# A planned order fitted anew: the planner counts TensorE's changes between full and half-array products, and has new lengths for attention's products

## The chip, the cores and the metric

The kernel runs on one core of a Trainium2 chip. The number to explain is the device time of one execution in microseconds. Before the change three runs took 861.77, 862.43 and 864.25 us; their median is 862.43.

The core's engines each take their own instructions strictly in order: TensorE (PE, matrix products; its weight loads are shown as PEld), VectorE (DVE), ScalarE (ACT), GpSimd (POOL), and SyncE (SP), which here only issues transfers. They meet through semaphores: an instruction that waits holds everything behind it on its engine.

## The reference

Attention with a window of 128 keys and a distance penalty per head, then two layers of a pair of products with a gate between them:

```python
# q, k, v: 4 batches, 8 heads, 576 positions, 64 per head
scores = scale * np.matmul(q, k.transpose(0, 1, 3, 2))
mask = (rel >= 0) & (rel < window)                       # window = 128
scores = np.where(mask, scores + bias[None], -1000000000.0)
attn = np.exp(scores - max) ; attn = attn / (sum + 1e-09)
x = matmul(attn, v), heads side by side                  # 2304 tokens x 512
h = x @ w_in ; g = h * np.tanh(softplus(h)) ; x = g @ w_out     # layer 0, d_ff 2048
h = x @ w_in ; g = np.where(h > 0, h, np.exp(h) - 1) ; x = g @ w_out   # layer 1
```

## The kernel before, in words

**The products.** Each of the four products of the two layers (2304 x 512 x 2048 and its counterpart) is done by a scheme of seven block products in place of eight (STEPS P1 to P7), with sums and differences of blocks of the operands and the results on DVE, ACT and POOL. Every operand is split into a high part in the short fp32r format and a low rest, and each block product is three matmuls (high-high, high-low, low-high). The inward products of layer 0 have 288 columns (tiles hA, hB, hC; `hidden`), those of layer 1 and both outward products 384 (tiles hA, hB, hC and oA, oB, oC; `hidden`, `outward`). One planned PE operation is a block of 6 (hidden) or 12 (outward) matmuls.

**Attention** is cut into 48 units (`unit`): batch, pair of heads, and one of three parts of the positions. A unit has scores (tile ps_s), a softmax on DVE and ACT (p, st), one or two transposes (ps_t, L822), masked copies (pt, L852), and values (ps_o, L870). The scores of parts 0 and 1 (L767) use 64 of the array's 128 rows, for two heads side by side; the values use 64 of its columns; scores of part 2 (L755), transposes and all products of the layers use the whole array. Going from one of these three ways to another is what the change calls a change of mode.

**Weights** come packed. They are joined from two words (raw, bits; L633 to L646), summed (sums), and split (w); those of layer 0's inward product stay on the core, the others go out to memory and come back later. Between the two products of a layer the gate (graw) goes through memory as well; its activation in layer 0 (L1020) needs another table of ACT than the joining of weights does (L635), and each alternation is an ACT_TABLE_LOAD.

**Stages.** Batch 0's attention runs first; from then on the attention of the next batch is interleaved with the hidden products of the one before (batches 0 to 3). The hidden products of batch 3 have no attention beside them. Then come layer 0's outward products (three blocks of 768 tokens), layer 1's hidden ones (three blocks) and layer 1's outward ones.

**Who sets the order.** The code first records every operation with its engine or engines, its modelled cost, what it reads and writes and when it is due (`Plan.op`, called by `pe`, `act`, `dve`, `dma`, `copy`, `combine`). `Plan.rank_all` gives each a priority: the due time of its users less its modelled step, plus the number that the table SHIFT has for its group (unit, weight tile, block product). `Plan.order` then plays the operations through on modelled engines: whenever an engine is free, it takes the ready operation of the lowest rank, and where several engines can do it, the one that would be done first. The instructions are emitted in the order so found; the modelled times themselves leave no trace in the program. When PE finds nothing ready in its model before the time AT["fill"] (90 us), it takes an unused product (L531: 256 columns in bf16, on a constant, which nobody reads), which keeps the engine active. The costs of PE's operations are written beside them: `pe(cost, ...)` at L755, L767, L822 and L870 for attention.

## Time and profile before

| | |
|---|---|
| median of three runs | 862.43 us (861.77 to 864.25) |
| the profiled execution | 861.93 us, its span 860.2 us |
| granted TensorE clock | 1.00 in every stretch looked at (of 2.4 GHz) |
| PE busy | 836.7 us, 97% of the span |
| DVE busy | 731.5 us, 85% |
| ACT busy | 617.9 us, 72% |
| POOL busy | 116.2 us, 14% |

A stretch is read by comparing its length with what each engine was busy in it. Ends of matmuls are modelled and matmuls overlap, so PE's busy time is at most a hint; the time from the start of one block of products to the start of the next is exact. A number in brackets at a row's end is the engine's idle time before it and what ended that idle time.

### The profile page before, as it was taken

The numbers are of one execution on the slowest core, as the hardware profiler recorded it, in microseconds if no ns is written. First come the engines' busy times: TensorE is split into PE (matmuls) and PEld (weight loads), VectorE is DVE, ScalarE is ACT, GpSimd is POOL, SyncE is SP. The second block draws the span as 40 slices with busy tenths as digits, with TensorE's granted clock in tenths as the row PEclk, the third lists the DMA queues.
The fourth block names the chain that finished last, engine by engine and source line by source line (L and its number), as shares of the span: only waits on it lengthen the run. The fifth ranks groups of instructions, "written<-read, shape, count | busy, mean of one in ns | idle before, by whom it ended". The sixth has DMA issues, their size and how long they took to land.

```text
span 860.2 us, 15671 instructions
## 1 busy us (share of the span) xinstructions
PE 836.7 (97%) x5394; PEld 790.2 (92%) x5394; DVE 731.5 (85%) x1629; ACT 617.9 (72%) x1397; POOL 116.2 (14%) x104
## 2 busy tenths in 40 slices
PE   9999999999999999999899999999999998999998
PEld 6777788888889999999899999999999998999998
DVE  8999997888888789998899988986787997887863
ACT  6989887778788879885986667987699763322442
POOL 0432101112101000345200323221000000000000
PEclk9999999999999999999999999999999999999999
DMA  7346648997988996864874877793367937236001
GB/s 279 126 134 223 224 161 250 320 307 243 315 281 285 337 314 240 273 214 136 284 254 133 273 245 269 256 320 142 142 215 249 357 137 255 92 110 225 33 19 55
DMA packets 85967, 187.66 MB, mean 218 GB/s; under 512 B 8577, under 2 KB 30081, under 8 KB 85889
## 3 DMA queue, kind: packets, MB, share of 16 engines
q1 hardware_dynamic: 85888, 186.68, 64.1%
q8 instruction: 42, 0.69, 0.3%
q14 instruction: 37, 0.29, 0.1%
HBM read 117.44 MB, written 69.21 MB: 217 GB/s over the span
## 4 chain that ended last, share of the span: by engine, by line
PE 60%; DMA 13%; DVE 12%; ACT 7%; issue 6%; POOL 1%; SPq 1%; ACTq 0%; DVEq 0%; POOLq 0%
PE hA L956 20%; PE hC L956 10%; PE oA L1043 9%; PE oC L1043 5%; PE hB L956 5%; DMA graw<-gate 4%; DVE hl L576 3%; PE ps_o L870 3%; DMA qkv<-in_qkv_dram 3%; PE ps_s L767 2%; DVE graw L576 2%; DMA raw<-in_w_dram 2%; DVE w L576 2%; PE oB L1043 2%; PE ps_t L822 2%
## 5 line engine op out<-in xcount | busy, mean ns | idle before, releaser
L956 PE MATMUL hA<-xt,w 128*128 128x288 f32 (+1 forms) x1344 | 231.5, 317 | 3.4 <-ACT g L571 1.8
L1043 PE MATMUL oA<-hl,w 128*128 128x384 f32 x1152 | 215.9, 338 | 5.8 <-DVE hl L576 3.7
L956 PEld LDWEIGHTS hA<-xt,w 128*128 128x128 f32 x1344 | 207.3, 188 | 9.7 <-ACT g L571 3.6
L1043 PEld LDWEIGHTS oA<-hl,w 128*128 128x128 f32 x1152 | 202.7, 188 | 9.2 <-DVE hl L576 6.5
L571 ACT ACTIVATE hl<-graw 128x768 fp32r<-128x768 f32 x145 | 121.1, 842 | 111.1 <-PE oA L1043 58.0
L576 DVE TENSOR_TENSOR hl<-graw,hl 128x768 fp32r<-128x768 f32 x168 | 166.6, 1005 | 28.4 <-ACT hl L571 27.7
L956 PE MATMUL hC<-xt,w 128*128 128x288 f32 (+1 forms) x672 | 119.3, 317 | 1.0 <-ACT xc L571 1.0
L1043 PE MATMUL oC<-hl,w 128*128 128x384 f32 x576 | 108.8, 339 | 1.7 <-DVE hl L576 1.0
L956 PEld LDWEIGHTS hC<-xt,w 128*128 128x128 f32 x672 | 104.3, 188 | 3.7 <-ACT xc L571 1.3
L1043 PEld LDWEIGHTS oC<-hl,w 128*128 128x128 f32 x576 | 101.6, 188 | 3.1 <-DVE hl L576 2.0
L576 DVE TENSOR_TENSOR graw<-graw 128x768 f32<-128x768 f32 x96 | 92.6, 980 | 9.0 <-DMA graw<-gate 4.7
L646 POOL TENSOR_TENSOR bits<-bits,raw 128x512 int32<-128x512 int32 x30 | 47.7, 1591 | 296.0 <-DVE bits L643 176.0
L571 ACT ACTIVATE g<-hA 128x288 f32<-128x288 f32 (+1 forms) x144 | 60.7, 434 | 22.7 <-PE hA L956 20.4
L787 ACT ACTIVATE p<-p,st 128x128 f32<-128x128 f32 x144 | 56.2, 395 | 10.6 <-DVE st L783 10.4
L956 PE MATMUL hB<-xt,w 128*128 128x288 f32 (+1 forms) x336 | 60.5, 316 | 0.4 <-ACT g L571 0.4
L576 DVE TENSOR_TENSOR w<-w 128x512 fp32r<-128x512 f32 x84 | 56.7, 698 | 1.6 <-ACT w L571 1.5
L1043 PE MATMUL oB<-hl,w 128*128 128x384 f32 x288 | 54.3, 338 | 1.1 <-DVE hl L576 1.1
L956 PEld LDWEIGHTS hB<-xt,w 128*128 128x128 f32 x336 | 52.7, 188 | 1.2 <-ACT g L571 0.8
L571 ACT ACTIVATE w<-w 128x512 fp32r<-128x512 f32 x82 | 49.5, 625 | 4.3 <-DMA w<-w_out 3.1
L1043 PEld LDWEIGHTS oB<-hl,w 128*128 128x128 f32 x288 | 50.8, 188 | 1.4 <-DVE hl L576 1.4
L938 ACT ACTIVATE e<-e 128x384 f32<-128x384 f32 x96 | 48.9, 536 | 0.6
L802 ACT ACTIVATE p<-p,st 128x128 f32<-128x128 f32 x124 | 41.1, 396 | 8.9 <-DVE st L797 8.8
(99 smaller groups left out, 1114.9 us busy)
## 6 DMA issues: line engine op xcount, KB each, us to landing
graw<-gate SPq DMA_DIRECT2D x96, 384.0 KB, 5.9
raw<-in_w_dram SPq DMA_DIRECT2D x64, 512.0 KB, 5.5
gate<-g SPq DMA_DIRECT2D x64, 288.0 KB, 4.5
gate<-g SPq DMA_DIRECT2D x48, 384.0 KB, 3.6
w<-w_out SPq DMA_DIRECT2D x56, 256.0 KB, 4.8
qkv<-in_qkv_dram SPq DMA_DIRECT2D x16, 512.0 KB, 5.4
w_out<-bits SPq DMA_DIRECT2D x32, 256.0 KB, 4.8
w<-w_in SPq DMA_DIRECT2D x28, 256.0 KB, 3.1
```

Of the source, the lines that this page charges most:

```text
L571: ways = [("act", act_cost(n, sbuf), lambda: nc.scalar.activation(o(), i(), AF.Copy), 0.0), ("dve", dve_cost(n, sbuf), lambda: nc.vector.t ...
L576: emit = lambda eng: eng.tensor_tensor(out=o(), in0=x(), in1=y(), op=op)
L646: add = lambda eng, raw=raw, bits=bits: eng.tensor_tensor(out=bits().bitcast(I32), in0=bits().bitcast(I32), in1=raw()[:, :, 0].bitcast(I32 ...
L767: nc.tensor.matmul(pss[j]()[:, n, w0:2 * P], qs()[rs, n * P:(n + 1) * P], ks()[rs, ko + w0:ko + 2 * P], start=n == 0, stop=True, skip_grou ...
L787: act(P, lambda n=n, j=j: nc.scalar.activation(prob()[:, n, j], prob()[:, n, j], AF.Exp, scale=-1.0, bias=st()[:, 0, n, j:j + 1], accum_ou ...
L802: ("act", act_cost(P, True, 1), lambda y=y, f=f: nc.scalar.activation(y(), y(), AF.Copy, scale=f()), AT["norma"]),
L822: nc.tensor.transpose(ps()[:, j], prob()[:, n, j], ident)
L870: nc.tensor.matmul(o()[j * D:(j + 1) * D, c0:c0 + math.prod(y.shape[1:])], vn()[:kr, n, j], y, start=n == 0, stop=n == nkb - 1, skip_group ...
L938: act(T, lambda: nc.scalar.activation(e(), e(), AF.Relu, scale=-1.0, bias=1.0), (), [e], due)
L956: nc.tensor.matmul(ps(), w()[:, a, wi, cs], x()[:, b, k], start=step in FIRST and k == 0 and m == 0, stop=k == 1 and m == 2, skip_group_ch ...
L1043: nc.tensor.matmul(bk[name, d](), w()[:, a, wi, cs], x()[:, b, k], start=step in FIRST and f + k == 0 and m == 0, stop=f + k == NQ - 1 and ...
```

## The change

The planner now knows three modes of PE's operations: 0 (whole array), 1 (scores of parts 0 and 1), 2 (values). An operation in another mode than the last one costs SWITCH = 0.09 us more in the model, and its rank is worse by AT["mode"] = 3.5. The modelled lengths of attention's products are replaced by others, each shorter: scores 0.95 and 1.16 us become 0.76 and 0.97, those of part 2 0.33 become 0.19; a pair of transposes 0.22 becomes 0.14; values of parts 0, 1 and 2 0.90, 1.16 and 0.58 become 0.715, 0.93 and 0.44. With these costs the table SHIFT (over 500 numbers) and six numbers of AT were fitted again. No operation of the computation is added or taken away.

```diff
@@ -19,106 +19,109 @@
-AT = dict(copy=2.27, both0=-0.71, both1=-8.32, both2=-3.61, turn=7.60436, held=102.159, fill=90, enough=1.5, norma=-0.5,
-          normp=2.42, kappa=1.35238, lag=0.940919, first=-64.52, unit=2.69, h1=50.67, chunk=70.1, lead=30.24, dt=1.35,
-          dma=-7.29047, conv=-27.63, wadd=-0.1, soft0=0, soft1=0, soft2=0, soft3=0, eq=4, ep=2, et=6, er=3, eb=0,
-          eraw=3, side0=1, side1=2, depth=4, ahead=-153.07, hb=5, lrot=2)
+AT = dict(copy=2.27, both0=-0.71, both1=-8.32, both2=-3.61, turn=2.59709, held=117.913, fill=90, enough=1.5, norma=-0.5,
+          normp=2.42, kappa=1.33691, lag=0.880417, first=-64.52, unit=2.69, h1=50.67, chunk=70.1, lead=30.24, dt=1.35,
+          dma=-5.30616, conv=-27.63, wadd=-0.1, soft0=0, soft1=0, soft2=0, soft3=0, eq=4, ep=2, et=6, er=3, eb=0,
+          eraw=3, side0=1, side1=2, depth=4, ahead=-161.724, hb=5, lrot=2, mode=3.49599)
 SHIFT = {
-    "H000P1": -15.5, "H000P2": 52.4, "H000P3": -45.1, "H000P4": -13.3, "H000P5": -21, "H000P6": -39.5, "H000P7": -1.9,
...
+    "H000P1": -19.1, "H000P2": -27.5, "H000P3": -67, "H000P4": -32.8, "H000P5": -26.3, "H000P6": -65.3, "H000P7": 0.1,
...
@@ -148,6 +151,7 @@
     WARM = 4.0
     START = dict(pe=0.75, act=1.9, dve=2.6, pool=2.6, sp=0.6)
     LOAD = 1.3
+    SWITCH = 0.09
     RATE, OUTSTANDING, LANDING = 390e3, 8, 1.9
     def __init__(self):
@@ -178,7 +182,7 @@
                 return t + span
             t = (k + 1) * self.TICK + 1e-9
-    def op(self, ways, reads=(), writes=(), at=None, due=None, moved=0, rows=1.0, table=None, port=False):
+    def op(self, ways, reads=(), writes=(), at=None, due=None, moved=0, rows=1.0, table=None, port=False, mode=0):
         deps, bufs = set(), {}
         me = len(self.ops)
         for what, wr in [(x, False) for x in reads] + [(x, True) for x in writes]:
@@ -200,7 +204,7 @@
             b.left += 1
             b.ops.append(me)
         self.ops.append(dict(group=self.group, ways=ways, deps=deps, bufs=list(bufs), at=at, due=due, moved=moved, rows=rows,
-                             table=table, port=port))
+                             table=table, port=port, mode=mode))
     def rank_all(self):
         ops = self.ops
@@ -248,7 +252,7 @@
         events = sorted(free.values())
         dma_free = held_until = 0.0
         landed = []
-        loaded = "exp"
+        loaded, mode = "exp", 0
         self.columns = {}
         out = []
@@ -261,7 +265,8 @@
         def rank(e):
             held = AT["held"] * (e == "dve" and free["pool"] > t + 0.3)
-            return lambda i: (ops[i]["prio"] + AT["turn"] * turns(i) + held * ops[i]["port"], i)
+            return lambda i: (ops[i]["prio"] + AT["turn"] * turns(i) + held * ops[i]["port"] +
+                              (AT["mode"] if e == "pe" and ops[i]["mode"] != mode else 0.0), i)
         def finish(e, cost, i, t):
             ahead = 0.0
@@ -314,6 +319,7 @@
                             out.append(self.fill[1])
                         else:
                             continue
+                        mode = 0
                         free[e] = self.clocked(t, self.fill[0], 1.0)
                         self.fills.append((t, free[e]))
                         heapq.heappush(events, free[e])
@@ -334,7 +340,10 @@
                         at = max(t, held_until)
                     if o["moved"] and len(landed) >= self.OUTSTANDING:
                         at = max(at, landed[-self.OUTSTANDING])
-                    end = self.clocked(t, way[1], o["rows"]) if e == "pe" else at + way[1] + self.LOAD * turns(best)
+                    if e == "pe":
+                        switch = self.SWITCH * (o["mode"] != mode)
+                        mode = o["mode"]
+                    end = self.clocked(t, way[1] + switch, o["rows"]) if e == "pe" else at + way[1] + self.LOAD * turns(best)
                     loaded = o["table"] or loaded
                     late = self.LATENCY[e]
                     self.log.append((e, best, at, end))
@@ -561,8 +570,8 @@
     def dve(n, emit, reads, writes, due, fast=False, extra=0, port=False):
         plan.op([("dve", dve_cost(n, fast, extra), emit, 0.0)], reads, writes, due=due, port=port or fast)
-    def pe(cost, emit, reads, writes, at, rows=1.0):
-        plan.op([("pe", cost + 0.003, emit, 0.0)], reads, writes, at=at, rows=rows)
+    def pe(cost, emit, reads, writes, at, rows=1.0, mode=0):
+        plan.op([("pe", cost + 0.003, emit, 0.0)], reads, writes, at=at, rows=rows, mode=mode)
     def dma(moved, emit, reads, writes, due, slow=1.0):
         plan.op([("sp", 0.43, emit, 0.0)], reads, writes, due=due, moved=moved * slow)
@@ -752,7 +761,7 @@
             if part == 2:
                 ps = buf(ring, (512,), F32, "ps_s")
                 r = rows(4)
-                pe(0.0017 * nk, lambda: nc.tensor.matmul(ps()[:, :nk], qs(), ks(), start=True, stop=True), [t], [ps], at)
+                pe(0.001 * nk, lambda: nc.tensor.matmul(ps()[:, :nk], qs(), ks(), start=True, stop=True), [t], [ps], at)
                 dve(r, lambda: nc.vector.copy_predicated(ps()[:, :r], own[:, :r], ps()[:, P:P + r]), ["own"], [ps], due)
                 heads = [(0, 0, lambda: ps()[:, :P], relt[:, pr], ("relt", pr), ps)]
             else:
@@ -767,7 +776,7 @@
                             nc.tensor.matmul(pss[j]()[:, n, w0:2 * P], qs()[rs, n * P:(n + 1) * P], ks()[rs, ko + w0:ko + 2 * P],
                                              start=n == 0, stop=True, skip_group_check=True)
-                pe((0.66 if part == 0 else 0.87) + 0.29, mm, [t], list(pss), at, rows=0.8)
+                pe(0.76 if part == 0 else 0.97, mm, [t], list(pss), at, rows=0.9, mode=1)
                 for j, ps in enumerate(pss):
                     if part == 0:
                         dve(P, lambda ps=ps: nc.vector.copy_predicated(
@@ -821,7 +830,7 @@
                 for j in range(w):
                     nc.tensor.transpose(ps()[:, j], prob()[:, n, j], ident)
-            pe(0.109 * w, mm, [(prob, (n, j)) for j in range(w)], [ps], at)
+            pe(0.108 * w - 0.08, mm, [(prob, (n, j)) for j in range(w)], [ps], at)
             if part == 2:
                 from_, mask = (lambda kr: ps()[:kr, 0].rearrange("p (j q) -> p j q", j=2)), keep[:, :, :TAIL]
                 dst = lambda pt, x, kr: pt()[:kr, x, 0].rearrange("p (j q) -> p j q", j=2)
@@ -871,9 +880,9 @@
                                          start=n == 0, stop=n == nkb - 1, skip_group_check=True)
             cols = 2 * TAIL if part == 2 else P * sum(w for _, w, _, _ in places)
-            cost = 0.00175 * cols + 0.03 * nkb + (0.3 if part == 2 else 0.17)
+            cost = (0.715, 0.93, 0.44)[part]
             pe(cost, mm, [(pts[pt], x) for x0, w, _, pt in places for x in range(x0, x0 + (1 if part == 2 else w))] + [t],
-               [o], at, rows=0.0018 * cols / cost)
+               [o], at, rows=min(1.0, 0.0018 * cols / cost), mode=2)
             x, k = xc
             copy(nq, lambda: x()[:, k, q0:q0 + nq], lambda: o()[:, :nq], [o], [[(x, k, 0)], [(x, k, 1), (x, k, 2)], [(x, k, 3)]][part],
                  at + 2, sbuf=False)
```

Counted over the whole orders: PE's products of the computation are the same; the unused products are 193 where there were 146, of which 175 (140) stand ahead of the first hidden product and 18 (6) behind it; changes of mode are 137 where there were 134; ACT's table loads behind the first are 12 where there were 14. Some operations that more than one engine can do have moved between DVE, ACT and POOL.

First place, PE, from attention of batch 0 to the first hidden product (hA). Before:

```order
L767 MATMUL ps_s<-qkv 128x128 x2
L767 MATMUL ps_s<-qkv 128x256 x2
L870 MATMUL ps_o<-pt,qkv 64x64 x4
L870 MATMUL ps_o<-pt,qkv 64x256 x2
L870 MATMUL ps_o<-pt,qkv 64x128 x4
L870 MATMUL ps_o<-pt,qkv 64x256 x2
L870 MATMUL ps_o<-pt,qkv 64x128 x2
L956 MATMUL hA<-xt,w 128x288 x6
L531 LDWEIGHTS const-bfloat16-1.0
L531 MATMUL unused<-const-bfloat16-1.0 128x256
```

In the change:

```order
L879 MATMUL ps_o<-pt,qkv 64x256 x2
L879 MATMUL ps_o<-pt,qkv 64x128 x2
L965 MATMUL hA<-xt,w 128x288 x6
L776 MATMUL ps_s<-qkv 128x128 x2
L776 MATMUL ps_s<-qkv 128x256 x2
L879 MATMUL ps_o<-pt,qkv 64x64 x4
L965 MATMUL hC<-xt,w 128x288 x6
L965 MATMUL hB<-xt,w 128x288 x6
L965 MATMUL hA<-xt,w 128x288 x6
L776 MATMUL ps_s<-qkv 128x256 x4
L540 LDWEIGHTS const-bfloat16-1.0
L540 MATMUL unused<-const-bfloat16-1.0 128x256
```

A scores step and a values step of 64 columns, which stood close ahead of the first hidden block, now stand behind it; the six unused products (each with its weight load) that stood right behind the first hA block now stand behind later scores (7 of them there, and 4 and 7 more behind the next hC blocks).

Second place, ACT in layer 0's outward stage, second block of tokens (graw: activation of the gate, L1020, L1029 in the change; raw: joining of weights, L635, L639, in the change L644, L648; hl: high part of an operand). Before:

```order
L639 ACTIVATE raw<-raw 128x512
L635 ACT_TABLE_LOAD
L635 ACTIVATE raw<-raw 128x512
L1020 ACT_TABLE_LOAD
L1020 ACTIVATE graw<-graw 128x768 x2
L571 ACTIVATE hl<-graw 128x768 x2
L639 ACTIVATE raw<-raw 128x512
L1020 ACTIVATE graw<-graw 128x768
L635 ACT_TABLE_LOAD
L635 ACTIVATE raw<-raw 128x512
L571 ACTIVATE hl<-graw 128x768 x2
L1020 ACT_TABLE_LOAD
```

In the change:

```order
L1029 ACT_TABLE_LOAD
L1029 ACTIVATE graw<-graw 128x768 x4
L580 ACTIVATE hl<-graw 128x768
L1029 ACTIVATE graw<-graw 128x768 x3
L580 ACTIVATE hl<-graw 128x768
L1029 ACTIVATE graw<-graw 128x768
L580 ACTIVATE hl<-graw 128x768 x3
L648 ACTIVATE raw<-raw 128x512
L644 ACT_TABLE_LOAD
L644 ACTIVATE raw<-raw 128x512
L580 ACTIVATE hl<-graw 128x768
L644 ACTIVATE raw<-raw 128x512
```

The activations of the gate, which alternated with single conversions and their tables, now stand together behind one load; the conversions follow behind the next.

Third place, DVE in layer 1's outward stage, first block of tokens, from taking the results out of banks oB to those of oA (y), with the sums of the gate's blocks (graw) and the low parts of operands (hl). Before:

```order
L576 TENSOR_TENSOR y<-oB,y 128x384 x2
L576 TENSOR_TENSOR hl<-graw,hl 128x768
L576 TENSOR_TENSOR graw<-graw 128x2x384
L576 TENSOR_TENSOR hl<-graw,hl 128x768
L576 TENSOR_TENSOR graw<-graw 128x2x384
L576 TENSOR_TENSOR hl<-graw,hl 128x768
L576 TENSOR_TENSOR graw<-graw 128x2x384
L576 TENSOR_TENSOR hl<-graw,hl 128x768
L576 TENSOR_TENSOR y<-oA,y 128x384 x2
L576 TENSOR_TENSOR hl<-graw,hl 128x768
```

In the change:

```order
L585 TENSOR_TENSOR y<-oB,y 128x384
L585 TENSOR_TENSOR hl<-graw,hl 128x768
L585 TENSOR_TENSOR y<-oB,y 128x384
L585 TENSOR_TENSOR w<-w 128x512
L585 TENSOR_TENSOR graw<-graw 128x2x384
L585 TENSOR_TENSOR hl<-graw,hl 128x768 x2
L585 TENSOR_TENSOR y<-oA,y 128x384 x2
L585 TENSOR_TENSOR hl<-graw,hl 128x768
```

Between the two, DVE had three sums of graw and four low parts; now it has one sum, the low part of a weight tile and two low parts (and one between the two takings of oB).

## Rows read from the trace of the kernel before

**Rows 1.** One line of the page: busy us (share of the span) x instructions.

```profile
PE 836.7 (97%) x5394; PEld 790.2 (92%) x5394; DVE 731.5 (85%) x1629; ACT 617.9 (72%) x1397; POOL 116.2 (14%) x104
```

**Rows 2.** Stretches: window, length; busy us (count) of PE, PEld, DVE, ACT, POOL; clock; DMA.

```profile
0.00:44.20 44.20, 42.20 (x368) 30.99 (x368) 40.16 (x205) 36.71 (x133) 11.62 (x19) 1.00 0.58 204
44.20:120.00 75.80, 70.11 (x546) 59.65 (x544) 71.84 (x261) 67.38 (x212) 17.39 (x15) 1.00 0.60 199
120.00:264.70 144.70, 142.29 (x1124) 124.56 (x1123) 124.04 (x457) 111.87 (x359) 18.60 (x17) 1.00 0.81 267
...
309.75:497.00 187.25, 182.42 (x1025) 179.59 (x1024) 174.49 (x214) 149.31 (x210) 41.49 (x28) 1.00 0.70 234
497.00:673.50 176.50, 175.37 (x995) 173.78 (x994) 142.46 (x252) 144.98 (x318) 27.04 (x25) 1.00 0.68 233
673.50:856.60 183.10, 179.27 (x1010) 176.68 (x1008) 144.58 (x182) 71.94 (x103) 0.00 (x0) 1.00 0.39 136
```

**Rows 3.** The chain that ended last, in order of time: start us, us, what.

```profile
733.51 10.53 PE oA L1043 x60
```

**Rows 4.** PE in order of time, 112 to 122 us: start us, us, what, count.

```profile
117.05 0.60 PE L870 MATMUL ps_o<-pt,qkv 128*64 128x64 f32 x8
117.58 1.07 PE L956 MATMUL hC<-xt,w 128*128 128x288 f32 x6
118.48 0.96 PE L956 MATMUL hB<-xt,w 128*128 128x288 f32 x6
119.28 0.96 PE L956 MATMUL hA<-xt,w 128*128 128x288 f32 x6
120.17 1.14 PE L767 MATMUL ps_s<-qkv 64*128 64x256 f32 x8
121.23 0.93 PE L956 MATMUL hC<-xt,w 128*128 128x288 f32 x5
```

**Rows 5.** The same view around the first hidden product; in brackets idle time before.

```profile
35.05 3.19 PE L531 MATMUL unused<-const-bfloat16-1.0 128*128 128x256 bf16 x27
38.08 0.27 PE L822 MATMUL ps_t<-ident,p 128*128 128x128 f32 x1
...
44.21 1.06 PE L956 MATMUL hA<-xt,w 128*128 128x288 f32 x6
45.11 0.84 PE L531 MATMUL unused<-const-bfloat16-1.0 128*128 128x256 bf16 x6
46.94 1.07 PE L956 MATMUL hC<-xt,w 128*128 128x288 f32 x6 [0.99 <-ACT xc L571]
```

**Rows 6.** DVE's groups by line and form: count | busy us, mean ns | idle before.

```profile
L576 DVE TENSOR_TENSOR w<-bits,w 128x512 fp32r<-128x512 f32 x11 | 8.5, 773 | 0.0
...
L646 DVE CUSTOM_DVE_ANT_0 bits<-raw,bits 128x1024 uint16<-128x1024 uint16 x34 | 24.8, 732 | 0.8
...
L576 DVE TENSOR_TENSOR sums<-sums,bits 128x256 f32<-128x256 f32 x21 | 9.0, 430 | 0.2
```

**Rows 7.** One of ACT's two kinds of table load, 404 to 422 us, same columns.

```profile
L1020 ACT ACT_TABLE_LOAD x2 | 2.6, 1283 | 0.0
```

**Rows 8.** PE in order of time, 404 to 422 us.

```profile
414.23 0.44 PE L1043 MATMUL oC<-hl,w 128*128 128x384 f32 x1 [0.66 <-ACT hl L571]
415.36 4.29 PE L1043 MATMUL oC<-hl,w 128*128 128x384 f32 x23 [0.69 <-DVE hl L576]
...
420.68 1.50 PE L1043 MATMUL oA<-hl,w 128*128 128x384 f32 x7 [0.86 <-DVE hl L576]
```

**Rows 9.** DVE in order of time, 712 to 730 us.

```profile
719.43 0.96 DVE L576 TENSOR_TENSOR graw<-graw 128x768 f32<-128x768 f32 x1 [1.97 <-DMA graw<-gate]
720.30 0.95 DVE L576 TENSOR_TENSOR hl<-graw,hl 128x768 fp32r<-128x768 f32 x1
```

**Rows 10.** PE in order of time, 712 to 730 us.

```profile
723.73 0.41 PE L1043 MATMUL oA<-hl,w 128*128 128x384 f32 x1 [1.52 <-DVE y L576]
724.97 2.20 PE L1043 MATMUL oA<-hl,w 128*128 128x384 f32 x11 [0.82 <-DVE hl L576]
```

191 rows, old and new, of the table SHIFT are left out of this document.

## Prediction

> **What bounds the kernel now.** I read the page's busy times first, then the stretches, then TensorE in order of time, then what its idle stretches wait for. The page gives PE 97% busy [rows 1], so the end is set by PE's queue: its products, its waits and its unused products. The change alters no product of the computation, so only the waits, the unused products and the joins between products can move. The reader is to see three kinds of stretch in [rows 2]. Up to 44.2 us PE holds attention products of the first batch and unused ones; it idles 44.20 - 42.20 = 2.0 us. From 44.2 to 120 it idles 75.80 - 70.11 = 5.7 us while DVE is busy 71.84 of 75.80: there DVE paces it. From 120 to 264.7 it idles 2.4 us, and in the outward stage of layer 0, layer 1's inward stage and its outward stage 4.8, 1.1 and 3.8 us. That is 19.8 us, a lower bound, since ends of matmuls are modelled and products overlap in the records. The upper bound for the last three stretches comes from the pitch: in the chain that ended last, 60 products of 384 columns stand in a row for 10.53 us [rows 3], 0.1755 us each; the order has 3024 of them in the 546.85 us from 309.75 on, 530.7 us, so 16.1 us are lost there, not 9.8. The granted clock is 1.00 in every stretch, so it is no term.
>
> **The change part by part.** (1) *Lengths.* The old planner gave the scores of a part-1 unit 1.16 us and the values of a part-2 unit 0.58. In [rows 4] these scores take 121.23 - 120.17 = 1.06 us and these values 117.58 - 117.05 = 0.53. The new figures, 0.97 and 0.44, give 1.06 and 0.53 with one change of mode added, so they are right here. A plan that holds PE some 0.1 us per attention step too long puts the work of the other engines too late by as much; this can be worth something only where PE, not DVE, is the pacer: from 120 to 264.7 us. What it is worth has no row; the ends are -2.4 us (all idle time there) and +2 us (as much again lost by a new order). I take -1.0, under half of the idle time, because a new order moves such waits as easily as it closes them.
>
> (2) *Changes of array mode.* Six hidden products between two other sixes take 119.28 - 118.48 = 0.80 us; ahead of a half-array product they take 120.17 - 119.28 = 0.89, behind one 118.48 - 117.58 = 0.90 [rows 4]. So a change costs 0.09 to 0.10 us, and 0.09 is the new planner's figure. The order has 137 changes where there were 134: +3 x 0.09 = +0.3 us. The Trainium skill states the same as a rule, in "TensorEngine Tiling (Array Packing)", Key Properties: "Changing tiling mode (not just tile) drains the TensorE". By that rule an order with more changes is the slower one, and this one has more; the trace agrees that each costs, and its 0.09 us makes the sum of the rule the same +0.3.
>
> (3) *Unused products and the start.* 47 more, 35 of them ahead of the first hidden product and 12 between the first few (the first piece of order in the section on the change). 27 take 38.08 - 35.05 = 3.03 us [rows 5], so 0.112 each: 5.3 us in all. What hides them is waiting: PE idles 2.0 us before 44.2 [rows 2], and 0.99 us behind the six unused ones after the first hidden product [rows 5]; the rest of the 5.7 us up to 120 is paced by DVE, so a PE that comes later there waits less. Below, all 5.3 us are covered and a better filling saves 1; above, nothing is covered. I take +0.8, near the lower end because DVE is busy 95% of that stretch. One scores step (0.85 with its change, by the new figures) and one values step (0.53) now stand behind the first hidden product; they only move.
>
> (4) *DVE's work up to the 24th unit's masks.* Counted in the orders, DVE has 439 instructions there where it had 445: 4 fewer additions of `bits` (732 ns), 7 fewer `sums` (430), 4 more `w` splits of 512 (773) [rows 6], and one split of `xt` fewer against one half-size `w` and one scaling of `raw` more, which I set equal. That is -2.9 - 3.0 + 3.1 = -2.8 us of durations; records of DVE overlap at their joints (one of 0.96 us is followed after 0.87 [rows 9]), so I take a tenth off: -2.5. PE has one block of six hidden products fewer ahead of that point (0.80 us), so what PE has to wait for DVE there falls by 1.7 us. The additions taken away go to POOL or come later; POOL is busy 17.39 of those 75.80 us [rows 2]. I take -1.2; the ends are 0 (POOL's result comes late) and -2.5.
>
> (5) *Activation tables.* In the second piece of order, ACT loads a table four times around a few `graw` before; now eight `graw` run behind one load, and the next load is for two conversions together. Over the program 14 switching loads become 12. Each is 1283 ns [rows 7]; two are 2.6 us of ACT, at the place where PE waits 0.66 + 0.69 + 0.86 = 2.2 us within 7 us, for `hl` of ACT and DVE [rows 8]. ACT is not PE's pacer elsewhere, so only this pocket counts: 0 to -2.6; I take -1.8. When that stall goes, the transfer of `graw` and DVE's own `hl` are next late.
>
> (6) *Layer 1, first token block.* In the third piece, DVE had three sums of `graw` and four `hl` splits between its two takings of oB and the takings of oA; now one sum, one weight split and two `hl`. PE waited 1.52 us for that y (the next product accumulates into the same bank), then 0.82 for `hl`, while DVE had itself waited 1.97 us for a transfer of `graw` [rows 9, 10]. Three instructions fewer of 0.87 us from start to start [rows 9] bring the taking of oA 2.6 us forward, if the transfer is not late then at an earlier sum. 0 to -2.3; I take -1.5. The waiting sum now stands ahead of oB's taking, with the `hl` of the running step behind it: that is what would wait instead.
>
> (7) *The pockets I did not compare.* Of the 9.8 us idle after 309.75, 4.5 are in (5) and (6). The other 5.3 are in single waits of 0.4 to 1.2 us. The refitted table moves nearly every instruction by a few places, so some of these close and others open: 0, with ends of 2.5 either way.
>
> **The sum.** -1.0 + 0.3 + 0.8 - 1.2 - 1.8 - 1.5 + 0 = -4.4 us. The profiled execution took 861.93 us (span 860.2, 1.7 around it, which nothing here alters); 861.93 - 4.4 = 857.5. It lies 0.5 below the median of the runs, 862.43, well inside their spread.
>
> **Rivals.**
> *The unused products are in the way* (slower). They are put where the plan sees PE idle; in an in-order queue they also run where the operands have already come. Its place is the start up to 47 us and its price 5.3 us, and it decides when the first hidden product starts more than 2 us after 44.2 and DVE is never idle before 120. For it: PE waited only 2.0 + 1.0 us at these places, less than the 5.3 to be hidden. Against it: the 95% of DVE. With nothing from (1) and (4), and half of (5) and (6): 861.93 + 5.3 + 0.3 - 1.6 = 865.9.
> *Waits only move* (no change). The pockets of (5) and (6) hang on transfers too: graw's are behind each other in one SP queue, and a DVE that saves 2.6 us arrives at the next sum as much earlier than its transfer. Then (5), (6) and (1) give nothing and (4) is taken up by (3): about 862. For it: the 1.97 us of DVE for a transfer; against it: ACT's loads are real work that goes.
> *It does not do what it says.* The changes are counted, and there are three more; if the order only trades one set of small waits for another, 861.9 + 0.3 = 862.2.
> *The new lengths fit everywhere.* All idle time from 120 to 264.7, both pockets and half of the rest go: 861.93 - 2.4 - 2.2 - 2.6 - 2.3 - 2.5 = 849.9. Against it: DVE stays as full as it was.
>
> **How the numbers follow.** Chances: the forecast has 0.49, the large gain 0.09, the two without change 0.17 and 0.08, the slower one 0.17. What can be told from no change is 0.3%, 2.6 us: faster is below 859.8, slower above 865.0. So faster 0.58, same 0.25, slower 0.17. The forecast's own range is 853 to 860. The whole one reaches down to the large gain's time, 850, and up to the slower rival's, 866; beyond these I leave 1 in 10 on each side.
>
> **What would show it.** (3): the first hidden product within 2 us of 44.2, PE's idle time before 120 smaller by what the unused ones take. (4): DVE's busy time from the first hidden product to the end of the second batch's masks lower by about 2 us, POOL's higher. (5): 12 switching loads in the page, no PE wait over 0.6 us among the `graw` of the second token block of layer 0. (6): no wait of PE for y in layer 1's first block. (2): hidden products beside half-array ones still 0.89. The forecast is wrong if the first hidden product is later than 46.5 us and that delay is still there at layer 0's outward stage, or if PE's idle time after 309.75 is as large as the 9.8 us of before.

## The result, and the profile after

| | before | change |
|---|---|---|
| median of four runs each | 862.10 us (860.78 to 864.25) | 855.07 us (853.35 to 855.64) |
| ratio | | 0.9913, 95% interval 0.9887 to 0.9938 |
| profiled execution, span | 861.93, 860.2 us | 855.64, 853.7 us |
| predicted | | 857.5 (850 to 866) |

The change is 7.0 us faster by the medians, 6.3 by the two profiled executions. The total was forecast well; its parts were not, as the profile shows. First PE's busy time, from the page of the change [against rows 1]:

```profile
PE 841.2 (99%) x5441; PEld 795.1 (93%) x5441; DVE 726.4 (85%) x1623; ACT 619.1 (73%) x1400; POOL 121.1 (14%) x105
```

The 47 more unused products are in PE's count, 5441 - 5394; its busy time is 4.5 us longer. The stretches of the change, with their ends near the same products as in [rows 2] (first hidden product, a point near 120 us, last batch's hidden products, first outward product, then the ends of layer 0's outward and of layer 1's inward stage); columns as in [rows 2]:

```profile
0.00:46.50 46.50, 44.69 (x387) 33.41 (x388) 39.62 (x201) 36.71 (x132) 10.22 (x19) 1.00 0.56 194
46.50:122.20 75.70, 72.02 (x563) 60.39 (x562) 72.48 (x257) 66.01 (x210) 22.83 (x20) 1.00 0.59 191
122.20:267.20 145.00, 143.69 (x1135) 126.31 (x1136) 127.87 (x465) 115.65 (x366) 18.10 (x14) 1.00 0.82 277
...
311.80:497.90 186.10, 184.38 (x1040) 181.94 (x1039) 169.51 (x214) 151.52 (x218) 43.05 (x29) 1.00 0.72 242
497.90:670.40 172.50, 172.27 (x977) 170.71 (x976) 138.06 (x245) 140.97 (x307) 24.05 (x22) 1.00 0.66 228
670.40:850.20 179.80, 179.33 (x1016) 177.84 (x1014) 142.69 (x180) 74.38 (x106) 0.00 (x0) 1.00 0.40 138
```

Two things are to be seen. The first hidden product starts at 46.50 where it started at 44.21, and the first outward one at 311.31 where it started at 309.76, with one block of hidden products (0.80 us) still to do behind it: up to there the change is slower. From there on PE idles 1.7, 0.2 and 0.5 us where it idled 4.8, 1.1 and 3.8. The granted clock is 1.00 in every stretch of both kernels and is no part of the difference.

What PE waited for from 309 us on, the longest rows in the kernel before (us in all, times, longest):

```profile
PE oA L1043 <- DVE hl L576: 3.7, 8, 0.9
PE oA L1043 <- DVE y L576: 1.5, 1, 1.5
PE hA L956 <- ACT g L571: 1.1, 1, 1.1
PE oB L1043 <- DVE hl L576: 1.1, 1, 1.1
PE oC L1043 <- DVE hl L576: 1.0, 2, 0.7
```

and in the change:

```profile
PE hA L965 <- DVE xt L585: 0.7, 1, 0.7
PE oA L1052 <- DVE hl L585: 0.6, 1, 0.6
PE oC L1052 <- DVE hl L585: 0.2, 1, 0.2
```

These rows hold 13 waits of 8.4 us before and three of 1.5 us in the change; with the shorter rows it is 15 waits of 9.6 us before and six of 2.1 in the change, and y appears in none of the change's.

For finer places the table below gives the **time lost up to a product block**: its start less the summed durations of the computation's products ahead of it (0.175 us for 384 columns, 0.133 for 288, attention's from rows like [rows 4]). It counts unused products, waits and joins alike. It is an estimate, but all kernels have the same products, so differences hold to some tenths. "Start" is up to the first hidden product, "attention" from there to the first outward one, then layer 0 outward, layer 1 inward and outward; the last two columns are 126 products each around the pockets of the prediction's terms (5) and (6), before from 392 to 417 and from 712 to 738 us. The kernels below the second line are the experiments.

| us lost | start | attention | out 0 | in 1 | out 1 | all | pocket (5) | pocket (6) |
|---|---|---|---|---|---|---|---|---|
| before | 21.5 | 22.2 | 8.1 | 2.5 | 6.2 | 60.5 | 3.2 | 3.2 |
| change | 25.1 | 21.0 | 4.4 | 1.7 | 2.2 | 54.4 | 0.6 | 0.3 |
| late_new | 20.9 | 23.7 | 10.3 | 1.6 | 2.3 | 58.8 | 0.1 | 0.9 |
| late_old | 24.9 | 20.8 | 7.7 | 4.3 | 7.1 | 64.8 | 3.3 | 4.0 |
| start_old | 21.2 | 22.8 | 4.1 | 2.1 | 1.9 | 52.1 | 0.5 | 0.3 |
| mid_old | 21.3 | 22.9 | 4.5 | 2.2 | 3.2 | 54.1 | 1.1 | 0.3 |
| few_fills | 24.9 | 21.9 | 3.8 | 2.1 | 2.3 | 55.0 | 1.1 | 1.1 |
| mid_fills | 24.4 | 22.7 | 4.1 | 2.3 | 2.0 | 55.5 | 0.8 | 0.7 |
| out0_new | 21.5 | 23.1 | 5.1 | 2.8 | 6.5 | 59.0 | 1.5 | 2.9 |
| out1_new | 21.6 | 22.7 | 8.8 | 2.8 | 1.6 | 57.5 | 3.3 | 0.4 |
| tables_late | 21.4 | 25.1 | 6.7 | 2.7 | 4.4 | 60.3 | 1.3 | 2.2 |
| y_first | 20.8 | 22.2 | 8.7 | 3.4 | 2.8 | 57.9 | 3.0 | 0.4 |
| costs_only | 24.8 | 27.6 | 18.0 | 3.5 | 7.1 | 81.0 | 2.3 | 2.4 |
| table_only | 24.5 | 30.2 | 9.1 | 9.5 | 5.7 | 79.0 | 0.9 | 0.9 |

Kernels that share an order in a column show how far one profiled execution can be trusted: where the order is before's, the start loses 20.8 to 21.6 us, attention 22.2 to 25.1, out 0 7.7 to 8.8, in 1 2.5 to 4.3, out 1 4.4 to 7.1, pocket (5) 3.0 to 3.3, pocket (6) 2.2 to 4.0.

Pocket (5) in the change, PE from 416 us on, as [rows 8]:

```profile
416.38 4.33 PE L1052 MATMUL oC<-hl,w 128*128 128x384 f32 x24
420.91 0.44 PE L1052 MATMUL oA<-hl,w 128*128 128x384 f32 x1 [0.20 <-ACT hl L580]
421.90 2.21 PE L1052 MATMUL oA<-hl,w 128*128 128x384 f32 x11 [0.55 <-DVE hl L585]
```

Three waits of 0.66, 0.69 and 0.86 us have become two of 0.20 and 0.55. Pocket (6), DVE and then PE, as [rows 9, 10]:

```profile
714.87 0.95 DVE L585 TENSOR_TENSOR graw<-graw 128x768 f32<-128x768 f32 x1
715.74 1.82 DVE L585 TENSOR_TENSOR hl<-graw,hl 128x768 fp32r<-128x768 f32 x2
717.48 1.01 DVE L585 TENSOR_TENSOR y<-oA,y 128x384 f32<-128x384 f32 x2
```

```profile
719.09 2.53 PE L1052 MATMUL oA<-hl,w 128*128 128x384 f32 x12
721.46 2.24 PE L1052 MATMUL oC<-hl,w 128*128 128x384 f32 x12
```

y is taken out of oA from 717.48 on, and PE's next oA block at 719.09 waits for nothing: 1.52 and 0.82 us are gone.

### The profile page after: what moved, and what is told of

It reads as the page before. It is cut to its first block, busy times and chain, and to the rows that moved or that the text cites. A ratio compares the mean times of both kernels' runs of the same rounds, so it can differ in the third digit from the quotient of the medians.

```text
span 853.7 us, 15782 instructions
## 1 busy us (share of the span) xinstructions
PE 841.2 (99%) x5441; PEld 795.1 (93%) x5441; DVE 726.4 (85%) x1623; ACT 619.1 (73%) x1400; POOL 121.1 (14%) x105
## 4 chain that ended last, share of the span: by engine, by line
PE 65%; DVE 14%; DMA 9%; ACT 5%; issue 4%; POOL 1%; SPq 0%; DVEq 0%; ACTq 0%; POOLq 0%
PE hA L965 21%; PE oA L1052 11%; PE hC L965 10%; PE hB L965 5%; PE oC L1052 5%; DVE hl L585 5%; PE ps_o L879 4%; DMA graw<-gate 4%; DVE graw L585 3%; PE ps_s L776 2%; PE oB L1052 2%; DVE w L585 2%; DMA qkv<-in_qkv_dram 2%; PE unused L540 2%; PE ps_t L831 2%
## 5 line engine op out<-in xcount | busy, mean ns | idle before, releaser
L580 ACT ACTIVATE hl<-graw 128x768 fp32r<-128x768 f32 x152 | 127.3, 843 | 107.4 <-PE oA L1052 50.6
L585 DVE TENSOR_TENSOR hl<-graw,hl 128x768 fp32r<-128x768 f32 x168 | 162.5, 979 | 35.5 <-ACT hl L580 34.6
L585 DVE TENSOR_TENSOR graw<-graw 128x768 f32<-128x768 f32 x96 | 90.4, 959 | 7.0 <-ACT graw L1029 4.2
L796 ACT ACTIVATE p<-p,st 128x128 f32<-128x128 f32 x144 | 56.2, 394 | 11.1 <-DVE st L792 10.9
L585 DVE TENSOR_TENSOR w<-w 128x512 fp32r<-128x512 f32 x84 | 59.0, 723 | 2.5 <-ACT w L580 2.0
L965 PE MATMUL hB<-xt,w 128*128 128x288 f32 (+1 forms) x336 | 60.3, 316 | 0.0
L1052 PE MATMUL oB<-hl,w 128*128 128x384 f32 x288 | 54.4, 338 | 0.2 <-DVE hl L585 0.2
L861 DVE TENSOR_TENSOR pt<-ps_t,keep 128x256 f32<-128x256 f32 (+2 forms) x128 | 43.4, 382 | 8.9 <-PE ps_t L831 8.4
```

The lines of the kernel that those rows point to most:

```text
L580: ways = [("act", act_cost(n, sbuf), lambda: nc.scalar.activation(o(), i(), AF.Copy), 0.0), ("dve", dve_cost(n, sbuf), lambda: nc.vector.t ...
L585: emit = lambda eng: eng.tensor_tensor(out=o(), in0=x(), in1=y(), op=op)
L796: act(P, lambda n=n, j=j: nc.scalar.activation(prob()[:, n, j], prob()[:, n, j], AF.Exp, scale=-1.0, bias=st()[:, 0, n, j:j + 1], accum_ou ...
L861: dve(w * P, lambda x=x, key=key, kr=kr: nc.vector.tensor_tensor(out=dst(key[0], x, kr), in0=from_(kr), in1=mask[:kr, x:x + 1].broadcast_t ...
L965: nc.tensor.matmul(ps(), w()[:, a, wi, cs], x()[:, b, k], start=step in FIRST and k == 0 and m == 0, stop=k == 1 and m == 2, skip_group_ch ...
L1052: nc.tensor.matmul(bk[name, d](), w()[:, a, wi, cs], x()[:, b, k], start=step in FIRST and f + k == 0 and m == 0, stop=f + k == NQ - 1 and ...
```

## The experiments

All kernels record the same operations. Most splice two finished orders, before's (0) and the change's (1): one is emitted up to a named product, then what is left in the other's order. H is the inward and O the outward stage; the digits are layer, block of tokens (in layer 0's H the batch) and, for H, unit, all counted from 0; the steps are planned in the order P1, P5, P6, P2, P7, P3, P4. The edits are shown in short form.

**The stages apart.** late_new has before's order up to layer 0's first outward product, late_old the opposite.

```diff
-    for emit in plan.order(): emit()
+    for emit in spliced(orders, [(0, "O00P1"), (1, None)]): emit()   # late_new
+    for emit in spliced(orders, [(1, "O00P1"), (0, None)]): emit()   # late_old
```

> The order of before up to layer 0's first outward product, the order of the change from there on (what had not been issued by then follows in the change's order). The two traces lie 2.4 us apart, the change behind, at that product's place (44.2 against 46.5 us at the first hidden product, 264.7 against 267.2 at batch 3's hidden ones), and the change gains 8.5 us behind it. Theory A, the stages are separable and all of the gain is in the outward and layer-1 stages: 862.1 - 8.5 = 853.6, a ratio of 0.990, and 1 to 2.5 us faster than the change. Theory B, the late gain depends on what the early order has left in buffers, transfers and conversions: about half of it, 857 to 859, ratio 0.995. Theory C, the attention's new lengths and counted modes make the gain: 862 to 864, no gain.

> The reverse: the change's order up to layer 0's first outward product, the order of before from there on. Theory A: 855.1 + 8.5 = 863.6, ratio 1.002 to 1.003 (the early part alone is a small loss). Theory B: 858 to 861. Theory C (the gain is made in the attention stages): 855 to 857, ratio 0.993.

Measured: late_new 861.00 us, ratio 0.9989 (0.9968 to 1.0010); late_old 865.84, ratio 1.0049 (1.0028 to 1.0069). late_new can't be told from before; its time lies between theories B and C and fits neither. It hides a gain: at the join, operands that the change's order would have prepared earlier are missing. PE there:

```profile
320.05 0.69 PE L1201 MATMUL oC<-hl,w 128*128 128x384 f32 x1 [2.89 <-ACT hl L725]
321.26 3.89 PE L1201 MATMUL oC<-hl,w 128*128 128x384 f32 x11 [0.52 <-DVE hl L730]
324.94 2.88 PE L1201 MATMUL oA<-hl,w 128*128 128x384 f32 x12
```

From the product that stands 75 us behind the first outward one to the end, where the join is over, late_new loses 7.4 us, the change 7.8, before 15.4. So the late part of the change is worth some 8 us behind either start, and in late_new the join took nearly all of it. late_old keeps before's late losses behind the change's start and is slower than both. Its 865.84 us are 2 us more than theory A's sum; they lie in layer 1 (4.3 and 7.1 us lost for before's 2.5 and 6.2), and their cause is open. The gain is late, and the early part brings none.

**The start.** start_old has before's order up to the first hidden product, mid_old up to batch 1's sixth hidden unit. In the trace of mid_old that join stands at 175 us; the 62 us of its expectation are wrong.

```diff
+    for emit in spliced(orders, [(0, "H000P1"), (1, None)]): emit()   # start_old
+    for emit in spliced(orders, [(0, "H015P6"), (1, None)]): emit()   # mid_old
```

> The order of before up to the first hidden product (140 unused products ahead of it), the change's from there on. Theory A1, the 2.3 us that the first hidden product comes later are lost for good: first hidden product at 44 to 44.5 us, 855.1 - 2.3 = 852.8, ratio 0.989. Theory A2, DVE paces the stretch to 120 us, so that a PE that is there earlier only waits longer: first hidden product at 44.2, but batch 1's hidden products where the change has them, 854.5 to 855.5, ratio 0.992.

> The order of before up to batch 1's sixth hidden unit (about 62 us), where the two orders have issued nearly the same operations, and the change's order from there; 142 unused products. Theory A2 (the change's loss of 2.3 us sits in its start, and before's order is the better one somewhat past the first hidden product too): first hidden product at 44 us, 851.5 to 853.5 us in all, as fast as or up to 2 us faster than the kernel that took before's order only to the first hidden product (853.5, ratio to before 0.990). Rival (a join inside the attention costs waits, since eight operations are out of step there): a wait of PE over 1 us near 62 us and 854 to 857.

Measured: start_old 853.52 us, ratio 0.9899 (0.9874 to 0.9923); mid_old 854.22, ratio 0.9897 (0.9870 to 0.9925). With before's start the first hidden product comes at 43.95, and 52.1 us are lost in all, 2.3 fewer than in the change. By ratio it is 0.14% better than the change, but the intervals overlap: the trace shows the 2 us, the times alone don't. mid_old isn't better than start_old, and no wait of PE over 0.6 us stands near its join. Up to the 85th hidden block (161 us) it has lost 1.4 us less than start_old (37.3 against 38.7), at the first outward product 0.2 more: what is gained there is lost again.

Why the change starts late is seen on DVE. From 30 to 46.5 us, in the change:

```profile
30.00:46.50 16.50, 16.50 (x154) 12.70 (x151) 13.82 (x61) 14.25 (x48) 6.63 (x7) 1.00 0.27 79
```

and up to there in start_old:

```profile
0.00:30.00 30.00, 28.81 (x236) 21.13 (x236) 26.39 (x149) 23.61 (x91) 4.21 (x12) 1.00 0.71 253
30.00:46.50 16.50, 15.60 (x144) 11.80 (x143) 16.01 (x69) 14.75 (x50) 8.25 (x8) 1.00 0.40 129
```

From 30 to 46.5 PE is busy without a gap in the change, and DVE only 13.82 of 16.50 us, with 8 instructions fewer done. What DVE waited for there is PE:

```profile
34.06 0.76 DVE L787 COPY_PREDICATED ps_s<-before,ps_s 128x256 f32<-128x256 uint8 x2 [0.85 <-PE ps_s L776]
...
42.17 0.42 DVE L861 TENSOR_TENSOR pt<-ps_t,keep 128x256 f32<-128x256 f32 x1 [0.60 <-PE ps_t L831]
...
45.59 0.48 DVE L861 TENSOR_TENSOR pt<-ps_t,keep 128x128 f32<-128x128 f32 x2 [0.73 <-PE ps_t L831]
```

From 10 to 46.5 us such waits of DVE for PE add up to 5.1 us in the change and to 0.3 in start_old.

**The unused products.** few_fills drops the change's last 47 (from 39.5 us on), mid_fills the 45 from 30.5 to 39.5 us.

```diff
+    if i is not None or seen <= 146: emit()              # few_fills
+    if i is not None or not 101 < seen <= 146: emit()    # mid_fills
```

> The change's order with its last 47 unused products left out, so that 146 stand as before: 29 ahead of the first hidden product, 18 behind it (5.3 us at 0.112 each). Theory D, they are in the way: the first hidden product comes 2 to 3 us earlier, at 43.5 to 44.5 us, and the whole is 852 to 853. Theory E, they fill waits for DVE and ACT: PE idles in their place, the first hidden product stays at 46 to 46.5 us, 854.5 to 855.5, ratio 0.992. If the granted clock falls without them: later than the change.

> The change without the 45 unused products that it has between 30.5 and 39.5 us (5 us of PE's time there); the others stay. Theory E2 (the unused products fill only waits; the start is late since PE has scores and values in an order in which DVE and ACT wait for PE and PE for them): the first hidden product stays within 0.5 us of 46.5, PE waits in those places instead, 854 to 857 us in all. Rival (unused products in the middle hold up scores that are already due, and DVE's waits of 0.85 and 0.73 us for PE come from them): the first hidden product comes 1 to 2.5 us earlier, at 44 to 45.5, and the kernel takes 852.5 to 854.5. A third way, told by the granted clock: the waits lower it and the products behind them take longer, 856 to 859.

Measured: few_fills 856.35 us, ratio 0.9932 (0.9905 to 0.9959); mid_fills 855.92, ratio 0.9909 (0.9881 to 0.9937). In few_fills the first hidden product comes 0.15 us earlier; PE waits instead, and what follows the waits is slow:

```profile
42.36 0.87 PE L1052 MATMUL ps_o<-pt,qkv 128*64 128x256 f32 x8 [0.68 <-DVE st L978]
44.45 0.33 PE L1003 MATMUL ps_t<-ident,p 128*128 128x128 f32 x1 [1.22 <-ACT p L983]
44.70 1.71 PE L1052 MATMUL ps_o<-pt,qkv 128*64 128x128 f32 x12
46.35 1.81 PE L1140 MATMUL hA<-xt,w 128*128 128x288 f32 x6
```

The same place in the change:

```profile
45.48 1.09 PE L879 MATMUL ps_o<-pt,qkv 128*64 128x128 f32 x12
46.50 1.06 PE L965 MATMUL hA<-xt,w 128*128 128x288 f32 x6
47.49 0.93 PE L776 MATMUL ps_s<-qkv 64*128 64x128 f32 x8
```

Twelve values products take 1.65 us from start to start where the change has 1.02, six hidden ones (to 48.09) 1.74 where it has 0.99. The granted clock of these stretches, in the last part of this text, says why. Without that the first hidden product would have come some 0.8 us earlier than in the change, not 0.15 (an estimate, 0.63 + 0.15), so few_fills is no clean test of what the unused products hold up.

mid_fills lies between its two expectations:

```profile
31.77 0.87 PE L1052 MATMUL ps_o<-pt,qkv 128*64 128x256 f32 x8 [0.52 <-DVE pt L1034]
...
36.10 0.56 PE L935 MATMUL ps_s<-qkv 128*128 128x192 f32 x2 [1.15 <-issue]
...
38.56 0.62 PE L1003 MATMUL ps_t<-ident,p 128*128 128x128 f32 x3 [0.88 <-ACT p L983]
...
45.87 1.06 PE L1140 MATMUL hA<-xt,w 128*128 128x288 f32 x6
```

PE waits 2.6 us in the bracketed rows for the 5 us taken away, and the first hidden product comes 0.6 us earlier (1.2, if one allows that this execution was 0.55 us late already in the scores ahead of them, at 28.42 for 27.87). So a part of the late start is theirs. It brings nothing to the end: at the first outward product mid_fills has lost 47.1 us, the change 46.1, and the ratios are 0.9909 and 0.9913. How much is left to the order itself is open. The two estimates, 0.8 and 1.2, together would be most of the 2.3 us, and no kernel leaves out both groups; but DVE still waits for PE 4.3 us in few_fills and 3.6 in mid_fills, from 10 to 46.5 us, and which operation stands too late was not tested by moving it.

**The two outward stages and the two pockets.** out0_new takes the change's order from the third step (P6) of layer 0's second outward block (382 us) to the last step (P4) of unit 5 in layer 1's last inward block (662 us), out1_new from there to the end. tables_late moves one weight conversion of before's order behind a run of `graw`, which leaves out two table loads; y_first moves three `graw` sums behind the taking of oA.

```diff
+    for emit in spliced(orders, [(0, "O01P6"), (1, "H125P4"), (0, None)]): emit()   # out0_new
+    for emit in spliced(orders, [(0, "H125P4"), (1, None)]): emit()                # out1_new
+    orders[0] = moved(orders[0], [c27 conversion], ahead_of=c30 conversion)        # tables_late
+    orders[0] = moved(orders[0], [3 graw sums of O11P5], behind=low part after y)  # y_first
```

> Before, but with the change's order from the third step of layer 0's second outward block to the last but one of layer 1's hidden units. Between these products the change gains about 3.5 us on before. Theory A: 862.0 - 3.5 = 858.5, ratio 0.996. Theory B: 860.5 to 862.

> The order of before up to the last but one of layer 1's hidden units (at a product where the two orders have issued nearly the same operations), the change's order from there on. From that place to the end PE of the change gains 4.0 us on before. Theory A: 862.0 - 4.0 = 858.0, ratio 0.995. Theory B (the gain hangs on what came earlier): 860 to 862.

> The order of before with one edit on ACT in layer 0's outward stage: one conversion of a weight (and what follows from it) is issued behind four more activations of the gate, right ahead of the next conversion, so that two of the 14 alternating table loads go. Theory 5, these loads (2.6 us of ACT) are what makes PE wait 0.66, 0.69 and 0.86 us there: those waits shrink to at most half, 859.8 to 861.0, ratio 0.998. Rival, ACT is not late because of them: the same waits, 861.5 to 862.5.

> The order of before with one edit on DVE in layer 1's outward stage: the three sums of graw for the second token block that stand between the taking of oB and the taking of oA in the first block are issued behind the taking of oA and the next low part. Theory 6, these sums (one of which waits 1.97 us for a transfer) are what makes PE wait 1.52 and 0.82 us there: PE's stall at 722 to 725 us goes, 859.7 to 860.3, ratio 0.9975. Rival, the wait moves to the next operands: a stall of 1.5 to 2.5 us within the next 15 us, 861.5 to 862.5.

| | us | ratio (95%) |
|---|---|---|
| out0_new | 860.41 | 0.9972 (0.9952 to 0.9991) |
| out1_new | 859.16 | 0.9961 (0.9945 to 0.9977) |
| tables_late | 860.97 | 0.9978 (0.9964 to 0.9993) |
| y_first | 859.64 | 0.9973 (0.9954 to 0.9991) |

All four are faster than before. out0_new and out1_new lie between their two expectations: 2.4 and 3.4 us of the 3.5 and 4.0 came. Of 862.4, tables_late's 0.22% is 1.9 us (0.6 to 3.1 by its interval), and its pocket loses 1.3 us where before's order loses 3.0 to 3.3; y_first's 0.27% is 2.3 us (0.8 to 4.0), its pocket 0.4 where before's order loses 2.2 to 4.0. PE in tables_late; only the last wait of [rows 8] is left:

```profile
416.88 4.39 PE L1227 MATMUL oC<-hl,w 128*128 128x384 f32 x24
421.11 0.34 PE L1227 MATMUL oA<-hl,w 128*128 128x384 f32 x1
422.32 2.21 PE L1227 MATMUL oA<-hl,w 128*128 128x384 f32 x11 [0.87 <-DVE hl L756]
```

PE in y_first, where [rows 10] has the waits of 1.52 and 0.82:

```profile
722.20 2.28 PE L1227 MATMUL oA<-hl,w 128*128 128x384 f32 x12
724.32 2.24 PE L1227 MATMUL oC<-hl,w 128*128 128x384 f32 x12
```

The transfer of `graw` that DVE had waited 1.97 us for does not become the new stall. The two moves make about 4.2 of the 8.5 us that the change gains behind the first outward product, if their gains add up (no kernel has both); what is left is not traced wait by wait, and the lists above hold only small ones for it.

**Costs without their table, and the table without its costs.**

```diff
+    orders = [planned(new_lengths=True, switch=0.09, table=OLD)]    # costs_only
+    orders = [planned(new_lengths=False, switch=0.0, table=NEW)]    # table_only
```

> The planner with the change's lengths of attention's products and its counting of mode changes (0.09 us in the model; the rank's 3.5 is off), but with before's table and its six numbers; 137 mode changes, 188 unused products. Theory C (the new costs by themselves bring nothing, the table is fitted to its costs and any other costs move it out of its fit): 864 to 880 us, with new PE waits in the stages behind the attention though no length was changed there. Rival (the truer lengths are what helps): 856 to 861 us.

> The planner with before's lengths and no counting of mode changes, but with the change's table and its six numbers; 137 mode changes, 184 unused products. Theory C (a table serves only the costs it was fitted with): 862 to 880 us. Rival (the gain lies in the table alone, and the new lengths only come along): 853 to 858 us.

Measured: costs_only 881.61 us, ratio 1.0215 (1.0181 to 1.0250), a little beyond the upper end expected; table_only 877.48, ratio 1.0168 (1.0136 to 1.0200). Each half by itself is far slower than either kernel. costs_only loses 28.6 us behind the first outward product, before 16.8, though the lengths differ in attention alone. Its longest wait is one that neither kernel has:

```profile
508.20 9.24 PE L1201 MATMUL oA<-hl,w 128*128 128x384 f32 x36 [4.75 <-DVE y L730]
517.28 1.20 PE L1114 MATMUL hC<-xt,w 128*128 128x384 f32 x6
```

So truer lengths and counted mode changes bring nothing with a table that was fitted to the old costs, and the new table nothing with the old costs: each table fits its own costs and not the other's.

## Why the prediction was right, and where it wasn't

The forecast took 4.4 us off the profiled time, the change 6.3. The sign is right and the time well inside the range. That it came so near is in part luck: the early terms (1) to (4) were 3.5 us too good (-1.1 forecast, +2.4 lost at the first outward product), the late ones (5) to (7) 5.2 too small (-3.3 for -8.5), and the two errors cancel. By steps:

- **(5) Activation tables, -1.8:** right. 12 switching loads, and tables_late alone is worth 1.9 us (0.6 to 3.1). In the change the pocket falls from 3.2 to 0.6, the term's other end.
- **(6) Three sums ahead of oA, -1.5:** right in its mechanism, too small. y_first gives 2.3 us by its ratio, the change's pocket 2.9, past the end of 2.3. The transfer for which I had held back was not late, and the pocket held smaller waits beside the two that I had added up.
- **(7) Uncompared pockets, 0 with ends of 2.5:** wrong in size. The stages behind the first outward product lose 8.3 us (8.3 = 4.4 + 1.7 + 2.2) for 16.8; less 2.6 and 2.9 for the two pockets, some 3 us were gained here. The new order closed more waits than it opened.
- **(3) Unused products and start, +0.8:** the step that failed. The start loses 25.1 us for 21.5, +3.6 (2.3 by the time of the first hidden product, the rest by the scores and values steps that now stand behind it), nearer the upper end of 5.3 than to +0.8. The unused products are a part of its cause: without 29 of them the delay stays, in part by the lower clock (few_fills), without 45 it shrinks by a quarter to a half and is back at the first outward product (mid_fills). What failed is the overlap: I read "DVE is busy 95%" and let a later PE cost little. Of the 3.9 us by which the change's start loses more than start_old's, attention gives back 1.8, and 2.1 are still lost at the first outward product. DVE was itself made to wait: up to 46.5 us it was busy 2.8 us less (39.62 by the first stretch above; start_old 26.39 + 16.01 = 42.40), and its waits for scores and transposes of PE were 5.1 us for 0.3.
- **(1) Lengths, -1.0, and (4) DVE's work, -1.2:** not borne out. Attention loses 21.0 us for 22.2, but that is the late start given back: with before's start it is 22.8 (start_old). DVE was busy 72.48 us in the second stretch, not 2 us less than 71.84; POOL took more, 22.83 for 17.39, as forecast. (1) to (4) were to give -1.1 and cost 2.4 us at the first outward product.
- **(2) Mode changes, +0.3:** its price holds. In the change six hidden products between two sixes take 115.15 - 114.36 = 0.79 us, ahead of values 116.05 - 115.15 = 0.90:

```profile
114.36 0.96 PE L965 MATMUL hB<-xt,w 128*128 128x288 f32 x6
115.15 0.96 PE L965 MATMUL hC<-xt,w 128*128 128x288 f32 x6
116.05 1.09 PE L879 MATMUL ps_o<-pt,qkv 128*64 128x128 f32 x12
```

The Trainium skill's "TensorEngine Tiling (Array Packing)", Key Properties, has the drain of TensorE behind such a change as a rule; the trace agrees, and gives it the price of 0.11 us here. Three more of them are too small a term to be seen in a run.

Of the rivals, *unused products in the way* named the right place and a late start, which it put at over 2 us (it was 2.3); how much of the cause it had is open, and it had no late gain above 1.6 us. *Waits only move* holds from 44 to 310 us and nowhere behind. *The new lengths fit everywhere* comes near the truth behind 310 us, where 2.4 us of idle time are left of 9.7, and not from 122 to 267, where 1.3 are left of 2.4 and attention's loss with before's start is not smaller (start_old). *It does not do what it says* is half true: there are more changes of mode, not fewer, and counting them brought nothing by itself (costs_only). My sign for a wrong forecast, a first hidden product later than 46.5 us and still felt at the outward stage, was all but met (46.50 us, and 2.4 us lost at that stage); the late gains were large enough to pay for it.

What stays open: whether a refit with the old costs would have found the same late order. The stages that gained hold no attention product, so no new cost enters there directly. It also stays open how the late start divides between the unused products and the order around them.

## What to carry to other kernels

Of this fitted order, neither the costs nor the table was worth anything alone: judge the finished order, pocket by pocket, where the trace of before shows waits, and expect waits that you did not look at to move as well. A pocket's gain can be tested by moving two or three operations of the old order. Where an engine is nearly full, ask what a new order makes that engine wait for, not only what waits for it.

## What the runs showed of the hardware

A wait of PE can cost more than itself. In late_new the granted clock is 1.00 from 300 to 310 us, where PE is busy throughout; behind PE's idle time of 2.89 us it is 0.50, the lower level of 1.2 GHz, from 320 to 325, and 1.00 again from 330 (columns as in [rows 2]):

```profile
300.00:310.00 10.00, 10.00 (x77) 10.00 (x76) 6.02 (x12) 5.68 (x13) 0.00 (x0) 1.00 0.84 291
310.00:320.00 10.00, 7.16 (x42) 6.85 (x41) 5.42 (x9) 3.89 (x7) 0.00 (x0) 0.97 0.93 310
320.00:325.00 5.00, 4.43 (x13) 4.03 (x14) 5.00 (x7) 4.97 (x8) 0.00 (x0) 0.50 1.03 409
325.00:330.00 5.00, 5.00 (x27) 5.00 (x26) 3.39 (x5) 5.00 (x8) 0.00 (x0) 0.87 1.05 398
```

The eleven products from 321.26 on last until the next block's start at 324.94, 3.68 us, where eleven take 1.93 at 0.1755 each. In costs_only, 36 products behind the wait of 4.75 us take 517.28 - 508.20 = 9.08 us for 6.32 (granted clock 0.59 from 510 to 515 us). In the change no stretch looked at is below 1.00. few_fills shows what the last of its unused products keep: without them the waits of 0.68 and 1.22 us come, and then

```profile
41.00:44.00 3.00, 1.55 (x12) 0.89 (x12) 3.00 (x11) 3.00 (x10) 2.02 (x2) 1.00 0.32 109
44.00:46.00 2.00, 1.55 (x13) 1.07 (x13) 1.66 (x5) 1.22 (x4) 0.00 (x0) 0.76 0.83 238
46.00:48.00 2.00, 2.00 (x10) 1.48 (x8) 1.31 (x4) 1.07 (x2) 0.00 (x0) 0.50 0.63 254
```

the clock is at its lower level from 46 to 48 us, and the 18 products read above take 1.38 us longer. That the array's clock has these two levels and falls when it idles, the Trainium skill's "TensorE: Matmul & The Clock Gate", Part 1, states as well; the trace agrees, and shows it fall where PE had idled in two pieces, neither of them above 1.3 us. In mid_fills the waits of 0.52, 1.15 and 0.88 us, further apart, left it at 1.00.
